# A hash-masked attention and gated MLP kernel: in 24 of 32 heads, VectorE instead of a DMA copies the rows of q and k that stay in their partitions

## The chip, the cores and the metric

The kernel runs on one core of a Trainium2 chip. The metric is device time in microseconds; before the change it is 724.53 us, the median of three runs (722.87, 724.53 and 728.32). The engines are called PE (TensorE), DVE (VectorE), ACT (ScalarE), POOL (GpSimd) and SP (SyncE, which here only issues DMAs).

## The reference

Four batches of eight heads, 768 positions, head dimension 64. A row of q may attend to those rows of k alone whose six-bit hash is the same; a row with no such partner attends to all of them alike. The attended heads of a batch go through a gated MLP with a spatial mixing matrix.

```python
q_bits = (np.einsum('bhsd,dk->bhsk', q, proj) > 0)          # 6 bits; k alike
mask = q_bucket[:, :, :, None] == k_bucket[:, :, None, :]
scores = np.where(mask, scale * (q @ k.T), -1e9)
attn = softmax(scores);  x = attn @ v                        # (B, S, H*D)
h = np.maximum(x @ w_in, 0);  u, v = h[..., :512], h[..., 512:]
v_n = (v - mean(v)) / sqrt(var(v) + 1e-6)
v_s = np.einsum('ts,bsd->btd', w_spatial, v_n) + b_spatial[None, :, None]
return (u * v_s) @ w_out
```

## The kernel before, in words

Every operand of a matmul that needs float32 accuracy is split into two float16 parts, high and low, and products of the parts are summed. Heads are numbered n = 0 to 31 and come in pairs p = n // 2, e = n % 2: one pair's q and k lie over each other in the 128 partitions, head e = 0 in partitions 0 to 63 and head e = 1 in 64 to 127.

For each pair, `load_qk` fetches k and q (768 KB), `hash_rows` makes the sign bits `sg` on PE and DVE, and `split_qk` writes the tile `hl`, four planes of 768 float16: q low, k high, q high, k low (L187 on ACT, L188 and L189 on DVE). There is one buffer for `hl`, so the split of the next pair waits until all that reads it is done.

For each head, `build` stacks these into one of four tiles `ab` of four planes: planes 0 and 1 hold q low over q high and k high over k low, so that one matmul over 128 partitions gives both cross products; planes 2 and 3 hold k high and q high in 64 partitions, and below them 12 rows of sign bits, with zeros (and in plane 2 a constant) under them. The rows of `ab` are brought by DMAs from SBUF to SBUF: one of 384 KB with the head's own 64 rows of four planes into partitions 0 to 63 (L210), one of 192 KB with two planes into partitions 64 to 127 (L211), and four small ones with the sign bits (L200), in the heads by queries from ACT's queue.

Heads 1 to 7 are done by keys (transposed scores, with a bound per row from `row_max` and its row 127 of `ab`); heads 0 and 8 to 31 by queries. A head by queries takes six steps of 128 queries. In a step, PE makes the scores (L291, L292), DVE takes the minimum of the negated scores into `nb` (L293), ACT the exponential (L294) and its float16 part (L297), DVE or POOL the rest (L298), SP issues a DMA transpose of the 384 KB `pp` into `pt` (L300), and PE multiplies by v (L313 to L315), at most five steps behind the scores. `normalize` and `transpose_x` end a head and a pair, and the MLP of a batch follows in 28 units that are spread over the 48 steps of the next batch; the last batch's MLP runs after the last step.

The order on each engine is set by a planner, which places instructions by the priority that `at(g, k)` gives and by its own timeline. In step g = 6n + i, `scores(n, i)` comes first; at i = 0, `build(n + 2)` is traced with priority 300 behind it, and what it puts on SP's queue is placed behind the last transpose (`tc.issue_after(st["tr"])`). `split_qk` of the pair after that comes at i = 3 of the odd head. SP's queue works in order: transposes, builds, loads, weights and outputs all pass through it.

Of the kernel before, what the change touches and what calls it, by code (L numbers as in the profile page):

```python
# [19 lines left out]
P = 128  # L20
D = 64
NB = 6
# [14 lines left out]
def lsh_attention_spatial_gating(  # L37
# [11 lines left out]
    nc = tc.nc  # L49
    B, NPAIR, _, _, S = kq.shape  # L50
    NH = 2 * NPAIR
    NT = S // P
    HS = S // 2
# [25 lines left out]


    NAB = 4
    NR = D + 2 * NB
    ab = [const.tile([P, 4, S], F16, name=f"ab{i}") for i in range(NAB)]
    for i, t in enumerate(ab):
        eng = nc.vector if i % 2 else nc.gpsimd
# [106 lines left out]
    def build(n):  # L192
        p, e = divmod(n, 2)
        hl, sg, t = st["hl", p], st["sg", p], ab[n % NAB]
        r = slice(D * e, D * e + D)
        q_s, q_h = (BQ_S[n >= NH], BQ_H[n >= NH])
        if n < 1:
            nc.sync.dma_start(out=t[0:D, 2:4], in_=hl[r, 1:3])
        for j in range(4):
            q_s.dma_start(  # L200
                out=t[D:NR, 3 - j // 2, (j % 2) * HS:(j % 2 + 1) * HS],
                in_=sg[32 * j + 16 * e:32 * j + 16 * e + 2 * NB, :])
        if n < 1:
            q_h.dma_start(out=t[0:D, 0:2], in_=hl[r, 0:2])
        else:

            top = hl[r, 0:2]
            (ps, pn), (ss, sn), (es, en) = top.ap
            src = replace(top, ap=[(ps, pn), (ss, 2), (ss, 2), (es, en)])
            q_h.dma_start(out=t[0:D].rearrange("p (a b) s -> p a b s", b=2), in_=src)  # L210
        q_h.dma_start(out=t[D:P, 0:2], in_=hl[r, 2:4])  # L211

    def split_v(p):
        if not has_queries(p):
# [40 lines left out]
    def scores_k(n, i):  # L255
        t = ab[n % NAB]
        ps = ps_sc.tile([P, 2, 512], F32, tag="sc", name=f"sp{n}_{i}")[:, :, :HS]
        ks = slice(i * P, (i + 1) * P)
        for c in range(2):
            cs = slice(c * HS, (c + 1) * HS)  # L260
            nc.tensor.matmul(ps[:, c], lhsT=t[:, 1, ks], rhs=t[:, 0, cs], start=True, stop=False)
            nc.tensor.matmul(ps[:, c], lhsT=t[:, 2, ks], rhs=t[:, 3, cs], start=False, stop=True)
        ex = wk.tile([P, S], F32, tag="pt", bufs=PTB, name=f"ex{n}_{i}")
        st["ex", n, i] = nc.scalar.activation(ex.rearrange("p (c q) -> p c q", c=2), ps, AF.Exp, scale=ISQ).ins
        st["pt", n, i] = ex
# [11 lines left out]
    def scores(n, i):  # L277
        if n in KEYS:
            scores_k(n, i)
            return  # L280
        t = ab[n % NAB]
        if i == 0:
            st["nb", n] = wk.tile([P, NT], F32, tag="nb", bufs=3, name=f"nb{n}")
        nb = st["nb", n][:, i:i + 1]
        ex = wk.tile([P, 2, HS], F32, tag="ex", bufs=EB, name=f"ex{n}_{i}")
        jk = ex.rearrange("p c k -> p (c k)").bitcast(BF16)[:, 0:S].rearrange("p (c k) -> p c k", c=2)
        qs = slice(i * P, (i + 1) * P)
        ps = ps_sc.tile([P, 2, 512], F32, tag="sc", name=f"sp{n}_{i}")[:, :, :HS]
        for c in range(2):
            cs = slice(c * HS, (c + 1) * HS)  # L290
            nc.tensor.matmul(ps[:, c], lhsT=t[:, 0, qs], rhs=t[:, 1, cs], start=True, stop=False)  # L291
            nc.tensor.matmul(ps[:, c], lhsT=t[0:P - 1, 3, qs], rhs=t[0:P - 1, 2, cs], start=False, stop=True)  # L292
        nc.vector.tensor_scalar(jk, ps, -ISQ, None, op0=ALU.mult, op1=ALU.min, accum_out=nb)  # L293
        st["ex", n, i] = nc.scalar.activation(ex, ps, AF.Exp, bias=nb, scale=ISQ).ins  # L294
        at(NT * n + i + G_H, 50)
        pp = wk.tile([P, 2, 2, HS], F16, tag="pp", bufs=PB, name=f"pp{n}_{i}")
        nc.scalar.copy(pp[:, 0], ex)  # L297
        (nc.gpsimd if i in (PL_POOL if n >= 2 * NH else PL_POOL1) else nc.vector).tensor_tensor(out=pp[:, 1], in0=ex, in1=pp[:, 0], op=ALU.subtract)  # L298
        pt = st["pt", n, i] = wk.tile([P, 2 * NT, P], F16, tag="pt", bufs=PTB, name=f"pt{n}_{i}")
        st["tr"] = nc.sync.dma_start_transpose(out=pt, in_=pp.rearrange("p g c k -> p (g c k)")).ins  # L300
# [183 lines left out]
    def at(g, k):  # L484
        tc.cur_priority = int(1000 * (g + 40) + k)
# [4 lines left out]
    hash_rows(0)  # L490
    split_qk(0)
    build(0)
    load_qk(1)
    build(1)
    load_v(0)
    at(-1, 0)
# [6 lines left out]
    for g in range(N * NT + LAG):  # L503
        n, i = divmod(g, NT)
        if n < N:
            at(g + G_S, 0)
            scores(n, i)
            r = n // 2
            at(g + G_P, 300)
# [17 lines left out]
            if i == BI and n + 2 < N:  # L527
                build(n + 2)
# [18 lines left out]
        while wv < N * NT and wv + (LAGK if wv // NT in KEYS else LAG) <= g:  # L547
            m, j = divmod(wv, NT)
# [64 lines left out]
```

## Time and profile before

| | |
|---|---|
| median of three runs | 724.53 us |
| the profiled execution, device time | 729.71 us |
| its span, first to last instruction | 727.9 us |
| granted PE clock, mean | 0.957 |
| busy: PE, DVE, ACT, POOL | 622.9, 520.4, 434.2, 326.6 us |
| DMA, bytes moved | 120.96 MB |
| DMA transposes of `pp` | 150 |
| DMAs of 384 KB into `ab` | 31 |

The profile comes from one execution. "Busy" of PE is modelled, since matmuls overlap; the DMA share is the mean busy share of 16 engines and can pass 1 where packets overlap. A wait is put down to what ended it last. Heads by keys fill about 49 to 165 us of the span, heads 8 to 31 about 165 to 650 us, and the last MLP the rest.

### The profile page before, as it was taken

The page shows a single profiled execution, that of the slowest core. Times are in us where ns is not written, and L with a number is a line of the kernel's source. Part 1 is how long each engine was busy: PE and PEld are TensorE (multiplying, and loading weights), DVE is VectorE, ACT ScalarE, POOL GpSimd, SP SyncE. Part 2 cuts the span into 40 slices and gives each one's busy share as a digit, 9 for nine tenths or more (in the row PEclk, how much of TensorE's full clock was granted, in tenths as well). Part 3 has the DMA queues.
Part 4 walks back from the last instruction along what each step waited for, and adds up shares of the span by engine and source line. Part 5 has one row for each costly group of instructions (what it writes and reads, how often), then busy time and mean ns, then how long its engine had stood idle before and what let it go on. Part 6 is the DMA issues. An engine that isn't in the chain of part 4 may idle for free. (4 is left out here: it accounts for less than half of the span.)

```text
span 727.9 us, 14930 instructions
## 1 busy us (share of the span) xinstructions
PE 622.9 (86%) x5759; PEld 393.2 (54%) x5759; DVE 520.4 (71%) x945; ACT 434.2 (60%) x668; POOL 326.6 (45%) x324
## 2 busy tenths in 40 slices
PE   1569897997987876998898899898989888999997
PEld 0237676875554543555555555565555555654553
DVE  4677894537899999768689887778699685845100
ACT  1345674356888677656667666667677677634221
POOL 5122542134479755446316672446146462441603
PEclk9969997999999988999999999999999999999999
DMA  9674745315999999997999999999999899860011
GB/s 238 151 140 146 170 132 105 94 47 131 233 247 210 212 198 203 218 210 161 223 213 186 193 202 183 228 197 206 228 227 169 167 168 210 147 157 10 1 44 44
DMA packets 290013, 120.96 MB, mean 166 GB/s; under 512 B 270741, under 2 KB 273813, under 8 KB 289941
## 3 DMA queue, kind: packets, MB, share of 16 engines
q1 hardware_dynamic: 287636, 119.11, 77.9%
q10 hardware_dynamic: 2304, 0.89, 0.5%
q8 instruction: 45, 0.74, 0.4%
q14 instruction: 28, 0.22, 0.1%
HBM read 28.33 MB, written 6.29 MB: 48 GB/s over the span
## 5 line engine op out<-in xcount | busy, mean ns | idle before, releaser
L294 ACT ACTIVATE ex<-sp,nb 128x768 f32<-128x768 f32 x150 | 134.6, 900 | 95.3 <-DVE ex L293 91.2
L293 DVE TENSOR_SCALAR_CACHE_REDUCE ex<-sp 128x768 bf16<-128x768 f32 x150 | 141.8, 949 | 43.2 <-PE sp L292 42.4
L298 DVE TENSOR_TENSOR pp<-ex,pp 128x768 f16<-128x768 f32 x116 | 125.9, 1091 | 20.7 <-ACT pp L297 20.5
L313 PE MATMUL pv<-vp,pt 128*128 128x65 f16 x900 | 105.5, 196 | 34.0 <-DMA pt<-pp 33.5
L291 PE MATMUL sp<-ab 128*128 128x384 f16 x300 | 102.2, 341 | 32.8 <-ACT ex L294 22.0
L297 ACT CAST pp<-ex 128x768 f16<-128x768 f32 x150 | 123.8, 830 | 10.6 <-ACT ex L294 2.5
L313 PEld LDWEIGHTS <-pt 128*128 128x128 f16 x900 | 85.4, 100 | 59.3 <-DMA pt<-pp 48.6
L298 POOL TENSOR_TENSOR pp<-ex,pp 128x768 f16<-128x768 f32 x34 | 58.2, 1711 | 123.9 <-ACT pp L297 101.1
L416 PE MATMUL sps<-ws,vn 128*128 128x384 f16 x576 | 103.9, 333 | 3.0 <-DVE sg L179 2.2
L314 PE MATMUL pv<-vp,pt 128*128 128x64 f16 x900 | 105.6, 195 | 0.0
L315 PE MATMUL pv<-vp,pt 128*128 128x65 f16 x900 | 105.3, 197 | 0.0
L292 PE MATMUL sp<-ab 127*128 127x384 f16 x300 | 102.4, 341 | 0.0
L314 PEld LDWEIGHTS <-pt 128*128 128x128 f16 x900 | 85.8, 99 | 10.7 <-issue 2.0
L315 PEld LDWEIGHTS <-pt 128*128 128x128 f16 x900 | 85.7, 99 | 3.7 <-issue 0.6
L416 PEld LDWEIGHTS <-vn 128*128 128x128 f16 x576 | 56.0, 100 | 40.7 <-issue 7.5
L431 PE MATMUL ops<-wo,g 128*128 128x512 f16 x288 | 70.0, 387 | 2.9 <-POOL wo L144 1.0
L401 PE MATMUL ups<-xt,wi 128*128 128x384 f16 x384 | 68.8, 331 | 0.0
L360 PE MATMUL vps<-wi,xt 128*128 128x512 f16 x288 | 67.1, 379 | 1.3 <-DMA xt<-xs 1.3
L332 POOL TENSOR_TENSOR x<-x,xf 128x384 f32<-128x384 f32 x32 | 36.8, 1151 | 69.7 <-DVE x L331 62.8
L274 PEld LDWEIGHTS pv<-vf,ex 128*128 128x128 f32 x504 | 65.6, 200 | 3.9 <-issue 1.1
L274 PE MATMUL pv<-vf,ex 128*128 128x65 f32 x504 | 64.5, 279 | 0.0
L421 POOL TENSOR_TENSOR sy<-sy,u 128x384 f32<-128x384 f32 x32 | 37.9, 1183 | 40.3 <-DVE sy L420 36.8
(87 smaller groups left out, 1006.1 us busy)
## 6 DMA issues: line engine op xcount, KB each, us to landing
qk<-kq SPq DMA_DIRECT2D x16, 768.0 KB
ab<-hl SPq DMA_DIRECT2D x31, 384.0 KB
ab<-hl SPq DMA_DIRECT2D x34, 192.0 KB
out<-o SPq DMA_DIRECT2D x24, 256.0 KB
v<-v SPq DMA_DIRECT2D x13, 384.0 KB
raw<-w_in SPq DMA_DIRECT2D x16, 256.0 KB
pt<-pp SPq DMA_TRANSPOSE x150
raw<-w_sp SPq DMA_DIRECT2D x12, 192.0 KB
```

The lines of the kernel that those rows point to most:

```text
L274: nc.tensor.matmul(acc[:, qi, :], lhsT=ex[:, qi * P:(qi + 1) * P], rhs=vf[p % 2][:, 2 * i + e, :], start=(i == 0 and qi == 0), stop=(i == ...
L291: nc.tensor.matmul(ps[:, c], lhsT=t[:, 0, qs], rhs=t[:, 1, cs], start=True, stop=False)
L292: nc.tensor.matmul(ps[:, c], lhsT=t[0:P - 1, 3, qs], rhs=t[0:P - 1, 2, cs], start=False, stop=True)
L293: nc.vector.tensor_scalar(jk, ps, -ISQ, None, op0=ALU.mult, op1=ALU.min, accum_out=nb)
L294: st["ex", n, i] = nc.scalar.activation(ex, ps, AF.Exp, bias=nb, scale=ISQ).ins
L297: nc.scalar.copy(pp[:, 0], ex)
L298: (nc.gpsimd if i in (PL_POOL if n >= 2 * NH else PL_POOL1) else nc.vector).tensor_tensor(out=pp[:, 1], in0=ex, in1=pp[:, 0], op=ALU.subtract)
L313: nc.tensor.matmul(acc, lhsT=pt[:, c, :], rhs=vh, start=(i == 0 and c == 0), stop=False)
L314: nc.tensor.matmul(acc[:, 0:D], lhsT=pt[:, c, :], rhs=vl, start=False, stop=False)
L315: nc.tensor.matmul(acc, lhsT=pt[:, NT + c, :], rhs=vh, start=False, stop=(i == NT - 1 and c == NT - 1))
L416: nc.tensor.matmul(ps[:, :HS], lhsT=vn[gv][:, c, d * P:(d + 1) * P], rhs=ws[gw][:, c, hs], start=(k == 0), stop=(k == 3 * NT - 1))
L431: nc.tensor.matmul(ps, lhsT=gt[h][gg][:, c, j * P:(j + 1) * P], rhs=wo[gw][:, c, :], start=(k == 0), stop=(k == 3 * NF - 1))
```

## The change

In the heads by queries from head 8 on (`near`), the head's own 64 rows stay in the partitions in which `hl` has them. Two DVE copies of 64 partitions by 1536 float16 bring the four planes there (k high and q high into planes 2 and 3; q low and k high into planes 0 and 1), and the DMA of 384 KB is gone. The two planes for the other half of the partitions are still brought by a DMA of 192 KB, and the sign bits by four small ones; in odd heads these now go to the lower half, since the head's own rows are in the upper half. For that the lower half of planes 2 and 3 of the two tiles that odd heads use is set to zero once by POOL, at heads 9 and 11, and the matmul of planes 3 and 2 takes all 128 partitions in odd heads. Head 0 and the heads by keys are built as before, and the minima are taken as before.

```diff
-    NR = D + 2 * NB
...
         q_s, q_h = (BQ_S[n >= NH], BQ_H[n >= NH])
+        near = n >= NH
+        z = D - D * e if near else D
+        if near and e and n < NH + NAB:
+            nc.gpsimd.memset(t[0:D, 2:4, :], 0.0)
...
             q_s.dma_start(
-                out=t[D:NR, 3 - j // 2, (j % 2) * HS:(j % 2 + 1) * HS],
+                out=t[z:z + 2 * NB, 3 - j // 2, (j % 2) * HS:(j % 2 + 1) * HS],
                 in_=sg[32 * j + 16 * e:32 * j + 16 * e + 2 * NB, :])
...
+        elif near:
+            nc.vector.tensor_copy(t[r, 2:4], hl[r, 1:3])
+            nc.vector.tensor_copy(t[r, 0:2], hl[r, 0:2])
         else:
...
-        q_h.dma_start(out=t[D:P, 0:2], in_=hl[r, 2:4])
+        q_h.dma_start(out=t[z:z + D, 0:2], in_=hl[r, 2:4])
...
+        K = P if n % 2 and n >= NH else P - 1
...
-            nc.tensor.matmul(ps[:, c], lhsT=t[0:P - 1, 3, qs], rhs=t[0:P - 1, 2, cs], start=False, stop=True)
+            nc.tensor.matmul(ps[:, c], lhsT=t[0:K, 3, qs], rhs=t[0:K, 2, cs], start=False, stop=True)
```

## The prediction

> **What bounds the kernel now.** I read the busy shares and the DMA row of the page first, then the chain that ended last, then the stretches between 165 and 650 us, in which the heads by queries run, and last the waits there.
>
> ```profile
> span 727.9 us, 14930 instructions
> PE 622.9 (86%) x5759; PEld 393.2 (54%) x5759; DVE 520.4 (71%) x945; ACT 434.2 (60%) x668; POOL 326.6 (45%) x324
> DMA  9674745315999999997999999999999899860011
> PE 14%; DMA 5%; POOL 4%; DVE 4%; issue 3%; ACT 2%; SPq 0%; ACTq 0%; POOLq 0%; DVEq 0%
> ...
> 490.83 0.24 POOL fl L323
> ...
> 520.47 4.86 DMA ab<-hl
> 525.35 1.49 ACT hl L187
> ...
> 653.02 3.29 DMA xt<-xs
> ```
>
> No engine is full over the span, and the DMA engines are full in nearly every slice in which queries run. The chain is known from 490.83 us on. Behind 653 us + 3.29 it is PE alone, the last MLP, which the change doesn't touch. Between 490.8 and 653 us, 162 us long, it changes hands all the time; the 4% of DVE are 29 us, so DVE holds 18% of that part (29 / 162), and once it runs through a DMA into `ab` for which ACT waited.
>
> ```profile
> core 0: us, PE busy (x) PEld busy (x) DVE busy (x) ACT busy (x) POOL busy (x), PEclk, DMA share, GB/s
> 50.00:165.00 115.00, 103.02 (x781) 82.41 (x780) 75.83 (x160) 59.75 (x106) 36.48 (x53) 0.93 0.47 117
> 165.00:650.00 485.00, 424.51 (x4451) 262.38 (x4449) 399.14 (x710) 337.78 (x504) 250.24 (x222) 0.96 0.98 198
> 200.00:300.00 100.00, 77.05 (x821) 47.27 (x820) 97.43 (x163) 76.68 (x133) 69.18 (x59) 0.93 1.03 214
> 375.00:400.00 25.00, 22.00 (x256) 14.18 (x254) 24.76 (x49) 18.73 (x32) 12.96 (x12) 1.00 0.94 197
> ```
>
> From 165 to 650 us DVE is busy 399.14 of 485 us (82%), PE 424.51 (88%), the DMA engines 0.98. In two stretches of 125 us together, DVE is busy 122.2: there each microsecond put on DVE lengthens the program. In the other 360 us DVE has 83 us of idle time.
>
> ```profile
> ACT ex L294 <- DVE ex L293: 77.2, 62, 3.6
> PEld L313 <- DMA pt<-pp: 40.8, 39, 3.8
> DVE ex L293 <- PE sp L292: 39.6, 29, 3.6
> PE sp L291 <- ACT ex L294: 22.0, 16, 2.6
> ...
> SPq L300 <- DVE pp L298: 71.9, 50, 6.2
> ...
> ACT hl L187 <- DMA ab<-hl: 8.7, 6, 2.2
> ```
>
> These are the waits between 165 and 650 us. PE waits for transposed `pt` 40.8 us in 39 of 144 steps: the largest wait of the engine that ends the program. SP waited for DVE's `pp` before 50 of the 144 transposes; the other 94 had their data ready (65%) and came when SP's queue let them. So the path through SP and the DMA engines, which the change relieves, and DVE, which it loads, are both near the limit.
>
> **The change, part by part.** *The DMA of 384 KB goes, in 24 heads.*
>
> ```profile
> L210 SPq DMA_DIRECT2D ab<-hl x22: 602/632/1488, 175.0 to 597.3; - x22
> ...
> L210 SPq DMA_DIRECT2D ab<-hl x2: 631/820/1010, 125.4 to 139.8; - x2
> ...
> ab<-hl SPq DMA_DIRECT2D x31, 384.0 KB
> ab<-hl SPq DMA_DIRECT2D x34, 192.0 KB
> ...
> 447.06 1.45 SPq L300 DMA_TRANSPOSE pt<-pp  x1
> ...
> 481.03 0.60 SPq L211 DMA_DIRECT2D ab<-hl  x1
> 481.80 2.79 SPq L300 DMA_TRANSPOSE pt<-pp  x1
> ...
> 500.69 0.60 SPq L211 DMA_DIRECT2D ab<-hl  x1
> 501.46 3.27 SPq L300 DMA_TRANSPOSE pt<-pp  x1
> ```
>
> Its issue takes SP 0.63 us (median). Further, a transpose that SP issues just behind a build takes 2.79 and 3.27 us to issue, against 1.45 us without one: 1.34 and 1.82, mean 1.58 us, in which the queue is still emptying. Of the 576 KB of a build 384 go, so I take two thirds, 1.05 us. SP's queue gains 0.63 + 1.05 = 1.68 us a head, 37 us over the 22 builds between 165 and 650 us (the two builds of such heads before, at 125 and 140 us, count nothing). As a cross-check, the DMA engines moved 117 GB/s at a share of 0.47 in the first stretch, 249 GB/s when full, which makes 1.58 us of 384 KB.
>
> How much of this reaches PE? I looked at the steps behind three builds.
>
> ```profile
>   PEld L313: 2.0, 1
> ...
>   PEld L313: 1.0, 1
> ```
>
> These are the waits on transposes issued at 464 to 471 us and at 501 to 505 us, both just behind a build; the one issued at 481.80 had no wait for it. With at most 1.68 us to be had at each, that is 1.68, 1.0 and 0: mean 0.89 us, times 22 heads 20 us, half of the 40.8 us. Its bounds are 0, if `pp` comes late instead, and 37 us. ACT's waits for these DMAs at L187 (8.7 us) shrink by two thirds, 5.8 us; ACT is busy 337.78 of 485 us and takes most of that up, so I count 2 us. Together **-22 us**.
>
> *Two DVE copies come, in 24 heads, 48 in all.* The trace has no such copy. The nearest row is L181, a DVE operation from float16 in SBUF to float16 in SBUF; L331 and L298 give the price of an operation that goes element by element.
>
> ```profile
> L181 DVE TENSOR_SCALAR sg<-sg,hc 128x384 f16<-128x384 f16 x16 | 8.9, 558 | 0.2
> L181 DVE TENSOR_SCALAR sg<-sg,hc x16: 302/320/1093, 11.2 to 560.0; 128x384 f16<-128x384 f16 x16
> L331 DVE TENSOR_TENSOR x<-pv,rv 128x384 f32<-128x384 f32 x32 | 17.7, 552 | 0.6
> L298 DVE TENSOR_TENSOR pp<-ex,pp x116: 921/954/1933, 34.2 to 643.9; 128x768 f16<-128x768 f32 x116
> L298 POOL TENSOR_TENSOR pp<-ex,pp x34: 1632/1646/2356, 26.3 to 632.9; 128x768 f16<-128x768 f32 x34
> ```
>
> 384 more elements cost 954 - 552 = 402 ns, 1.05 ns each, with 150 ns fixed. L181 takes 320 ns, 170 above the fixed part; four times as many elements make 680 + 150 = 0.83 us. At 1.05 ns an element the copy would take 1.76 us, the upper end; as the lower end I take 0.55 us, the 552 ns of L331, which has a quarter of the elements. L181's mean lies 0.24 us over its median, and its longest is 1.09 us: something holds it up at times. Operations of POOL last up to 1.65 us, and POOL is busy 250 of the 485 us. I take 0.83 + 0.24 = 1.07 us a copy, by the row most alike: 2.14 us a head, 47 us over 22 heads.
>
> The Trainium skill, VectorE: DVE Perf Modes, section "The perf-mode tier table", has 693 ns for a 16-bit copy of 2048 elements in SBUF; with its four elements a cycle that makes some 0.56 us here, an estimate from that page, and the sum below would be 5 us lower. Its page SBUF — State Buffer, section "Who interferes with whom", speaks against the change: such a copy needs a port pair that it shares with GpSimd, the one that comes second waits for the whole of the other's instruction. By that rule L181's longest time is a wait for POOL, which the trace allows, and POOL would wait for the copies too; the 0.24 us hold DVE's side of it.
>
> What does it cost? Five of the builds lie in the two stretches in which DVE is full (four from 200 to 300 us, one from 375 to 400):
>
> ```profile
> L210 SPq DMA_DIRECT2D ab<-hl x4: 627/632/802, 212.1 to 280.7; - x4
> ...
> L210 SPq DMA_DIRECT2D ab<-hl x1: 637/637/637, 380.5 to 380.5; - x1
> ```
>
> There 5 x 2.14 = 10.7 us count in full. Of the other 17 x 2.14 = 36.4 us I count DVE's share of the chain, 18%: 6.5 us. Together **+17 us**. If DVE's idle time is no cover at all, it is 47 us.
>
> *Behind the copies* stand DVE's minimum and difference of the next steps, which ACT, POOL and SP wait for (77.2 us of ACT's waits are for L293 already). They land on the steps whose transposes wait for SP now, so part of their delay is spent where the data lay ready anyway; that is why I don't charge them in full. The copies themselves wait for nothing: `hl` was split some three steps before, and the tile was last read by the head two before. L187 of the next split now waits for the odd head's copies as well, three steps later, which is covered.
>
> *Small parts.* Two fills by POOL, of heads 9 and 11:
>
> ```profile
> L86 POOL MEMSET ab<- 64x1536 f16 x2 | 2.7, 1374 | 0.1
> L291 PE MATMUL sp<-ab 128*128 128x384 f16 x300 | 102.2, 341 | 32.8 <-ACT ex L294 22.0 <-DMA ab<-hl 9.5 <-DVE mx L242 1.2
> L292 PE MATMUL sp<-ab 127*128 127x384 f16 x300 | 102.4, 341 | 0.0
> ```
>
> Each is the shape of L86, 1.37 us. The odd head's sign DMAs wait for it on ACT's queue, and ACT's exponentials stand behind them, for these two heads alone; POOL's queue may hold another 1.65 us. I count 0, with 3 us at most. The matmul over 128 rows costs what that over 127 does (341 ns each). The sign DMAs are as many and as large as before.
>
> The sum is -22 + 17 = **-5 us**: 724.7 us for the profiled execution, whose time was 729.7 (the span and 1.8 us around it). That execution was 5.2 us above the median of the runs, so for the median it makes 719.5 us, which I round to 720.
>
> **The rivals.** *The queue is the limit* (faster). What speaks for it: 65% of the transposes found their data ready, and the DMA share is 0.98. Then 65% of the 37 us of queue time reach PE, 24 us, and 2 us of ACT's; and with so much slack behind DVE its 47 us cost only the 18%, 8 us: -18 us, 706. Against it: DVE's full stretches, in which a shorter queue brings nothing.
>
> *DVE becomes the bound* (slower). From 165 to 650 us DVE is busy 399.1 us and waits 39.6 us for scores, which leaves 46.3 us; over the 44 copies, that is 1.05 us each. From there on, each further microsecond of a copy lengthens the stretch. At 1.5 us, between L181's price and the upper end, it is 66 - 46.3 = +20 us, 744; at 1.2 us, +6.5 us, 731. For it: my own price stands at this point. Against it: the 39.6 us of waits for scores shrink where PE waits less for `pt`.
>
> *An even exchange* (no change). The delay moves from SP's queue to DVE, in the same steps, and PE waits as long as before: 0 us, 724.5. For it speaks that a transpose starts at the later of SP and `pp`, and that 50 of 144 wait for `pp` already. My forecast lies near it. That the change does nothing at all is excluded by the DMA rows, since 24 transfers go.
>
> **The numbers.** A difference under 1%, 7.2 us, is about what a measurement of this kernel can't tell from none. Forecast and even exchange, both within 1%: 0.39 together (0.22 and 0.17). The queue as the limit, and what of the forecast's spread passes -7 us: 0.37. DVE as the bound, and an order of the planner that puts the copies ahead of urgent minima: 0.24. The range is 703 to 738: below, the first rival less the 3 us by which runs scatter; above, DVE as the bound at about 1.35 us a copy (59 - 46 = +13). Both signs hold much of the chance; the forecast alone spans 714 to 727.
>
> **What the profile after would show.** 7 DMAs of 384 KB into `ab` instead of 31; transposes behind a build issued in about 2 us instead of 2.8 to 3.3; PE's waits for `pt` near 20 us instead of 40.8; 48 copies of 0.55 to 1.2 us; DVE over 90% busy from 165 to 650 us. The forecast is wrong if the copies take over 1.2 us, if SP's waits for `pp` grow as much as its issues shrink, or if PE's waits for `pt` nearly vanish.

## The result, and the profile after

The changed kernel takes 730.4 us (median of 20 runs), the kernel before 727.47 us in 20 runs beside them. The ratio is 1.0066, with a 95% interval of 1.0038 to 1.0095: slower by 0.66%, some 5 us, where I had forecast 0.6% faster. Ratios, here and below, are taken over the fast runs alone, so this one is a little larger than the 2.9 us between the two medians would make it. The interval does not contain "no change", though the size is within the 1% I had called hard to tell. The profiled execution after took 730.83 us.

From the page of the kernel after: its span, the busy times, the DMA share in 40 slices, the chain that ended last, and the two kinds of DMA into `ab`.

```profile
span 729.0 us, 14947 instructions
PE 627.9 (86%) x5759; PEld 395.7 (54%) x5759; DVE 554.2 (76%) x993; ACT 434.2 (60%) x668; POOL 329.4 (45%) x326
DMA  9674644115969688694998978997987688860011
PE 16%; POOL 3%; DMA 3%; issue 2%; DVE 2%; ACT 1%; SPq 0%; POOLq 0%
...
ab<-hl SPq DMA_DIRECT2D x34, 192.0 KB
ab<-hl SPq DMA_DIRECT2D x7, 384.0 KB
```

The 24 transfers are gone and the DMA engines are no longer full. PE issues the same 5759 matmuls and is busy 5 us longer; DVE 33.8 us longer. The stretch of the heads by queries, and the two parts of it in which DVE was full (window, then busy us of PE, its weight loads, DVE, ACT and POOL, the granted clock, the DMA share and GB/s):

```profile
165.00:650.00 485.00, 427.81 (x4441) 263.42 (x4440) 429.89 (x751) 337.39 (x503) 251.06 (x223) 0.95 0.85 180
200.00:300.00 100.00, 74.94 (x735) 44.31 (x734) 97.79 (x163) 69.87 (x121) 66.83 (x58) 0.85 0.79 176
375.00:400.00 25.00, 20.75 (x213) 11.70 (x206) 23.73 (x49) 17.05 (x25) 7.15 (x7) 0.94 0.93 175
```

Between 200 and 300 us PE finished 735 matmuls instead of 821, its clock granted 0.85 instead of 0.93. The waits from 165 to 650 us (us, times, longest):

```profile
ACT ex L301 <- DVE ex L300: 84.8, 60, 4.7
...
PEld L320 <- DMA pt<-pp: 36.1, 38, 4.1
...
DVE ex L300 <- PE sp L299: 20.6, 21, 4.4
PE sp L298 <- ACT ex L301: 20.1, 18, 2.8
...
SPq L307 <- DVE pp L305: 119.6, 64, 7.4
```

PE's waits for `pt`, of which I expected half to go, fell by 4.7 us only. SP's waits for DVE's `pp` rose from 71.9 to 119.6 us, ACT's for DVE's minimum from 77.2 to 84.8. SP's queue itself did become free. Behind two builds of the kernel after (start, us to issue):

```profile
484.99 0.58 SPq L217 DMA_DIRECT2D ab<-hl  x1
485.73 1.44 SPq L307 DMA_TRANSPOSE pt<-pp  x1
...
504.83 0.59 SPq L217 DMA_DIRECT2D ab<-hl  x1
505.63 1.85 SPq L307 DMA_TRANSPOSE pt<-pp  x1
```

The 18 transposes that come next behind a build in SP's queue, from 165 to 650 us, took 2.94 us to issue in the median before and 1.57 after. The copies were cheaper than I had priced them (busy us, mean ns of one, idle time before them):

```profile
L209 DVE COPY ab<-hl 64x1536 f16<-64x1536 f16 x24 | 19.3, 803 | 0.2
L210 DVE COPY ab<-hl 64x1536 f16<-64x1536 f16 x24 | 18.2, 758 | 1.9 <-PE sp L267 1.7
```

A copy took 0.55 us in the mean where no operation of POOL ran at the same time (27 of the 48), and 1.08 us where one did (21).

So the relief is there and the price is lower than forecast, yet the sum has the other sign. DVE's own order of time (start, us) shows where the copies went:

```profile
198.17 0.94 DVE L187 SCALAR_TENSOR_TENSOR hl<-qk,hl 128x768 f16<-128x768 f32 x1
199.03 1.76 DVE L188 SCALAR_TENSOR_TENSOR hl<-qk,hl 128x768 f16<-128x768 f32 x1
200.71 1.18 DVE L209 COPY ab<-hl 64x1536 f16<-64x1536 f16 x1
201.82 0.17 DVE L376 BATCH_NORM_AGGREGATE mv<-bs 128x2 f32<-128x6 f32 x1
202.01 1.07 DVE L209 COPY ab<-hl 64x1536 f16<-64x1536 f16 x1
203.12 1.56 DVE L305 TENSOR_TENSOR pp<-ex,pp 128x768 f16<-128x768 f32 x1
204.60 1.84 DVE L210 COPY ab<-hl 64x1536 f16<-64x1536 f16 x2
206.47 0.96 DVE L300 TENSOR_SCALAR_CACHE_REDUCE ex<-sp 128x768 bf16<-128x768 f32 x1
```

The planner doesn't place two copies at each head's `build`. In eleven of the twelve pairs all four come close behind the split of that pair, about steps 3 to 5 of an odd head: they are done 3 to 9 us after its last operation starts, with two minima or `pp` between them at most. From 198.17 to 206.44 us, over 8 us, DVE makes one `pp` and no minimum. What PE does meanwhile (columns as above):

```profile
202.60:206.00 3.40, 3.40 (x47) 1.95 (x42) 3.35 (x4) 1.04 (x2) 2.85 (x3) 1.00 0.01 3
206.00:209.40 3.40, 1.59 (x24) 1.01 (x23) 3.34 (x7) 1.33 (x4) 0.00 (x0) 1.00 0.51 116
209.40:219.70 10.30, 6.54 (x40) 3.28 (x37) 10.13 (x24) 8.36 (x14) 6.63 (x5) 0.50 0.95 217
219.70:230.00 10.30, 9.21 (x115) 6.28 (x114) 9.45 (x15) 9.65 (x19) 9.71 (x10) 1.00 0.97 206
```

PE still has work until 206 us; the DMA engines, with no `pp` to transpose, are empty (0.01). Then PE works 1.59 of 3.40 us, and its clock is granted at 0.50 for the next 10.3 us: 40 matmuls, where the same time behind it holds 115. The stop that the burst brings is followed by a longer stretch at half clock.

### The profile page after: what moved, and what is told of

Its sections match the earlier page's. It is cut to its first block, busy times and chain, and to the rows that moved or that the text cites. A ratio compares the mean times of both kernels' runs of the same rounds, so it can differ in the third digit from the quotient of the medians.

```text
span 729.0 us, 14947 instructions
## 1 busy us (share of the span) xinstructions
PE 627.9 (86%) x5759; PEld 395.7 (54%) x5759; DVE 554.2 (76%) x993; ACT 434.2 (60%) x668; POOL 329.4 (45%) x326
## 5 line engine op out<-in xcount | busy, mean ns | idle before, releaser
L305 DVE TENSOR_TENSOR pp<-ex,pp 128x768 f16<-128x768 f32 x116 | 127.4, 1102 | 18.8 <-ACT pp L304 18.3
L320 PE MATMUL pv<-vp,pt 128*128 128x65 f16 x900 | 106.8, 197 | 28.6 <-DMA pt<-pp 28.1
L298 PE MATMUL sp<-ab 128*128 128x384 f16 x300 | 104.2, 347 | 30.9 <-ACT ex L301 20.1
L322 PE MATMUL pv<-vp,pt 128*128 128x65 f16 x900 | 106.7, 198 | 0.0
L423 PE MATMUL sps<-ws,vn 128*128 128x384 f16 x576 | 102.3, 331 | 4.6 <-DVE sy L427 4.6
L299 PE MATMUL sp<-ab 127*128 127x384 f16 (+1 forms) x300 | 104.6, 349 | 0.0
```

What stands on the lines that cost most here:

```text
L299: nc.tensor.matmul(ps[:, c], lhsT=t[0:K, 3, qs], rhs=t[0:K, 2, cs], start=False, stop=True)
L320: nc.tensor.matmul(acc, lhsT=pt[:, c, :], rhs=vh, start=(i == 0 and c == 0), stop=False)
L322: nc.tensor.matmul(acc, lhsT=pt[:, NT + c, :], rhs=vh, start=False, stop=(i == NT - 1 and c == NT - 1))
L423: nc.tensor.matmul(ps[:, :HS], lhsT=vn[gv][:, c, d * P:(d + 1) * P], rhs=ws[gw][:, c, hs], start=(k == 0), stop=(k == 3 * NT - 1))
```

## The experiments

My theory after the result: the relief is as large as forecast; the copies cost what they do because four of them close together (the "burst" below) hold back the minima and differences on which ACT, SP and so PE depend, where I had thought them covered. The rivals: it is only DVE's total load, wherever the copies stand; the copies block GpSimd at a port they share; or the planner's new order of everything else costs the time. Ratios are to the kernel before, with 95% intervals; 1% is 7.27 us, and differences in us are worked out from the ratios. Where two kernels are compared, the ± joins their intervals.

**Without the copies.**

```diff
         elif near:
-            nc.vector.tensor_copy(t[r, 2:4], hl[r, 1:3])
-            nc.vector.tensor_copy(t[r, 0:2], hl[r, 0:2])
+            pass
```

> The changed kernel without its 48 VectorE copies: the own rows of the heads by queries from head 8 on are not brought at all (they keep what lay there), so that neither the 384 KB DMA nor the copies run; all else is the same. It shows what the DMA was worth by itself, and, against the changed kernel, what the copies cost. Theory A (VectorE's load: the relief is real and the copies eat it): ratio to the kernel before 0.970 to 0.980, 15 to 22 us faster. Theory B (the four copies of a pair stand in one burst behind its split; their place costs more than their load): also 0.970 to 0.980. Theory C (the DMA was hidden and PE's waits for pt come from elsewhere): 0.995 to 1.005, and the copies then cost some 5 us.

Measured: 708.77 us, ratio 0.9762 [0.9707, 0.9816], that is -17.3 us. The relief, then, is real and near my 22 us, and the copies take 22 us (3.04% ± 0.6) for the 37.5 us that they last. Without them, ACT's waits for DVE are down by 29 us from the kernel after:

```profile
ACT ex L300 <- DVE ex L299: 55.5, 52, 2.7
PEld L319 <- DMA pt<-pp: 32.1, 28, 4.9
```

**Each copy twice.**

```diff
             nc.vector.tensor_copy(t[r, 2:4], hl[r, 1:3])
             nc.vector.tensor_copy(t[r, 0:2], hl[r, 0:2])
+            nc.vector.tensor_copy(t[r, 2:4], hl[r, 1:3])
+            nc.vector.tensor_copy(t[r, 0:2], hl[r, 0:2])
```

> The changed kernel with each copy made twice, so that 37 us more of VectorE time stand in the same places. Theory A: each further microsecond of VectorE costs about as much as the first ones, so 15 to 25 us over the changed kernel, ratio to the kernel before 1.027 to 1.04. Theory B: a burst of eight costs more than twice a burst of four: over 1.04. Theory C: 3 to 8 us over the changed kernel, ratio 1.01 to 1.018.

Measured: 753.58 us, 1.037 [1.0322, 1.0418]. The second set costs 22 us again (3.04% ± 0.6). There was no cover for the first set that the second has used up: as far as two points can tell, the cost runs straight from the first copy on. The copying lasts 65.1 us in all, 27.7 more (0.68 us a copy in the mean), so a microsecond of the second set costs more, not less.

**The copies spread.** One behind the minimum of step 1, one behind that of step 2, of the head two before.

```diff
+    def own_rows(n, d, s):
+        p, e = divmod(n, 2)
+        r = slice(D * e, D * e + D)
+        nc.vector.tensor_copy(ab[n % NAB][r, d:d + 2], st["hl", p][r, s:s + 2])
...
+            if i in (1, 2) and NH <= n + 2 < N:
+                with (tc.issue_after(st["mn", n, i]) if n not in KEYS else ExitStack()):
+                    own_rows(n + 2, *((2, 1) if i == 1 else (0, 0)))
```

> The changed kernel with its copies spread: one copy behind the minimum of step 1 and one behind that of step 2 of the head two before, so that no two copies stand next to each other and none stands behind the split. Theory A: the load is the same, so the time is that of the changed kernel, ratio 1.003 to 1.010. Theory B: PE's waits at the steps 0, 4 and 5 fall back to what they were before the change, and the relief of SP's queue stays: ratio 0.980 to 0.993. Theory C: 0.998 to 1.006.

Measured: 723.62 us, 0.9953 [0.9922, 0.9984]. This lies between the ranges of the theories. The copies are as many and as large, and the kernel takes 8 us less (1.13% ± 0.4). But they also last less, 31.7 us in all instead of 37.5 (0.78 us in the mean beside an operation of POOL, not 1.08); at 22 us for 37.5 that makes 3.4 of the 8 us. The rest points at the place, and the kernels in the old order, below, show it. PE's waits for `pt` end below those of the kernels so far (before 40.8, after 36.1, without copies 32.1). That wait, and the group of the copies:

```profile
PEld L324 <- DMA pt<-pp: 28.7, 27, 2.9
...
L221 DVE COPY ab<-hl 64x1536 f16<-64x1536 f16 x48 | 31.5, 660 | 2.4 <-PE sp L271 1.7
```

**The copies on ScalarE, and on GpSimd.** The second kernel has `nc.gpsimd.tensor_copy` at the same place.

```diff
-            nc.vector.tensor_copy(t[r, 2:4], hl[r, 1:3])
-            nc.vector.tensor_copy(t[r, 0:2], hl[r, 0:2])
+            nc.scalar.copy(t[r, 2:4], hl[r, 1:3])
+            nc.scalar.copy(t[r, 0:2], hl[r, 0:2])
```

> The changed kernel with the 48 copies on ScalarE, whose copy of as many elements takes about 1.5 us (its cast of 1536 float32 does): some 70 us more on an engine that was busy 70% of the time from 165 to 650 us, and nothing more on VectorE. Theory A: VectorE is relieved, ScalarE has the room: 0.980 to 0.995. Theory B: the burst stands on ScalarE instead and holds up the exponentials by 6 us each pair: 1.000 to 1.015. Theory C: 0.995 to 1.005.

> The changed kernel with the 48 copies on GpSimd, where a fill of as many elements took 1.37 us: 65 to 80 us more on an engine that was busy 52% of the time from 165 to 650 us. Theory A: VectorE loses the load, GpSimd has the room: 0.980 to 0.995. Rival (GpSimd's operations hold VectorE's two-input operations up, and its own differences and sums of x come late): 1.000 to 1.020.

Measured: 757.02 us, 1.0429 [1.0372, 1.0486], and 792.24 us, 1.0867 [1.082, 1.0914]. Both are slower than any theory had it. One copy lasts 1467 ns on ScalarE and about 1850 on GpSimd. The rows of the kernel with ScalarE, groups first, then waits:

```profile
L210 ACT COPY ab<-hl 64x1536 f16<-64x1536 f16 x24 | 35.2, 1467 | 0.0
```

```profile
PEld L320 <- DMA pt<-pp: 62.0, 40, 3.8
```

ScalarE is less busy than DVE (337 against 430 of 485 us in the kernel after), and yet its 70 us of copies cost 48 us over the kernel without copies. And this is no burst of four: by its trace, the planner put them on ScalarE two by two, some 20 us apart. An engine's spare time over the stretch doesn't say what more work on it costs.

**Fills instead of copies.** As in the kernel without copies, but DVE makes a fill that reads nothing for each, behind the split, as long as a copy with nobody in its way.

```diff
-            nc.vector.tensor_copy(t[r, 2:4], hl[r, 1:3])
-            nc.vector.tensor_copy(t[r, 0:2], hl[r, 0:2])
+            with tc.issue_after(st["s2", p]):
+                nc.vector.memset(spare[r], 0.5)
+                nc.vector.memset(spare[r], 0.5)
```

> The kernel without copies and without the 384 KB DMA, with a fill of 64x560 float16 by VectorE in a spare tile in place of each copy, placed behind the split as the copies are. A fill of 768 elements took 698 ns in the profile, so each should take about 0.55 us, the copy's shortest time, and reads nothing. It leaves out the own rows of the heads from 8 on. Theory A1 (what counts is VectorE's time alone): 26 us at 0.6, 16 us over the kernel without copies (0.976): 0.992 to 1.002. Theory A2 (what counts is the copy's way through a port shared with GpSimd: its waits, 0.23 us each of 0.78, and GpSimd's): under 0.987.

Measured: 745.36 us, 1.0238 [1.0195, 1.0281], 35 us above the kernel without copies and outside both ranges. The fills last less than the copies, and read nothing:

```profile
L211 DVE MEMSET spare<- 64x560 f16 x24 | 12.6, 525 | 2.8 <-issue 1.9 <-DVE spare L211 0.2
```

They cost more than the copies, so what a copy reads isn't the cause. But planned anew the fills may stand elsewhere, and this needed the four kernels that follow.

**The order of before, held.** In all kernels so far the planner had also reordered everything else: going by tile and shape, 3833 of PE's 5759 matmuls stand in the same place of its order after the change. In the next four, every engine is tied to its order in the kernel before; the copies go in behind the split of their pair (or spread as above), the 24 DMAs are gone. The order of the matmuls in all four traces is that of the kernel before, 5759 of 5759. In 6 of the 12 pairs the four copies behind a split stand in a row; in the others a minimum comes between the even head's two and the odd head's two, in some with more beside it. With relief alone and with fills, the own rows are left out.

```diff
+        info = mybir.DependencyInfo(mybir.DependencyClass.NoSync, mybir.DependencyReason.DATA)
+        for a, b in zip(order, order[1:]):
+            tc.add_manual_dep(b, a.name, info, reason="order")
...
+            if WORK in ("copies", "spread"):
+                i = nc.vector.tensor_copy(t[r, d:d + 2], hl[r, s:s + 2])
+            elif WORK == "fills":
+                i = nc.vector.memset(spare[r], 0.5)
```

> The instructions of every engine held in the order that the planner gave the kernel before; the 24 DMAs of 384 KB are gone and nothing brings the own rows of the heads from 8 on (they are left out). It is the relief of SP's queue by itself, without a new plan. Theory A (relief and load are both real, the plan matters little): as in the freshly planned kernel without copies, 0.971 to 0.982. Theory P (a good part of what was seen is the planner's new order): 0.985 to 1.000.

> The whole change in the order of the kernel before: the four copies of a pair stand behind its split on VectorE (those of the odd head not before the last minimum of the head that used the tile), everything else in the old order. Theory A: the same as the changed kernel, 1.000 to 1.012, that is some 20 us over the kernel with the relief alone. Theory P (the new order is what cost the gain): 0.983 to 0.995.

> As f2_copies_old_order, with a fill of 64x560 float16 of 0.53 us in a spare tile in place of each copy, in the same places (the own rows from head 8 on are left out). Theory A1 (VectorE's time is what costs): 25 us of fills and some 6 us of gaps at 0.6: 18 us over f1_relief_old_order, nearly as slow as f2_copies_old_order. Theory A2 (the port that the copies share with GpSimd is what costs): under 8 us over f1_relief_old_order. Theory P: the earlier run with fills, 35 us over the kernel without copies, owed its time to its plan, so in the old order it is within 10 us of f1_relief_old_order.

> As f2_copies_old_order, with the copies spread: one behind the minimum of step 1, one behind that of step 2 of the head two before. Theory A: the same as f2_copies_old_order, within 0.4%. Theory B (bursts): 5 to 10 us faster than f2_copies_old_order, 0.99 to 1.00 of the kernel before, or less.

| in the old order | us | ratio | against relief alone |
|---|---|---|---|
| relief alone, no copies | 705.99 | 0.9714 [0.9668, 0.9759] | |
| copies behind the split | 732.8 | 1.0103 [1.0047, 1.0159] | +28.3 us (± 5) |
| fills behind the split | 740.57 | 1.0176 [1.0131, 1.022] | +33.6 us (± 5) |
| copies spread | 721.16 | 0.9924 [0.9893, 0.9955] | +15.3 us (± 4) |

Waits from 165 to 650 us, of relief alone, of copies behind the split and of copies spread, in this order. (The profiled execution of the second took 740.86 us, the longest of its six, so its rows overstate the mean.)

```profile
ACT ex L355 <- DVE ex L354: 67.8, 55, 3.6
...
PE sp L352 <- ACT ex L355: 20.7, 14, 2.9
...
PEld L374 <- DMA pt<-pp: 19.6, 24, 2.4
...
SPq L361 <- DVE pp L359: 79.7, 48, 7.0
```

```profile
ACT ex L355 <- DVE ex L354: 88.9, 58, 5.0
...
PE sp L352 <- ACT ex L355: 33.9, 22, 5.4
...
PEld L374 <- DMA pt<-pp: 22.3, 22, 2.4
...
SPq L361 <- DVE pp L359: 105.5, 60, 8.4
```

```profile
ACT ex L355 <- DVE ex L354: 72.8, 65, 3.6
...
PE sp L352 <- ACT ex L355: 25.7, 17, 3.0
PEld L374 <- DMA pt<-pp: 26.3, 30, 3.1
...
SPq L361 <- DVE pp L359: 102.7, 57, 7.4
```

Three things follow. First, the relief alone is 20.8 us, and PE's waits for `pt` fall to 19.6 us, as the prediction said. Copies make SP wait longer for `pp` (26 us more in a burst, 23 spread), but the burst brings back hardly any of PE's waits for `pt` (22.3). What grows on PE's side is another wait: ACT waits 21 us more for the minimum, and PE 13 us more for ACT to have read the scores, so that their PSUM buffer is free. Spread, both grow by 5 us only.

Second, the place counts: the same copies, 33.7 us in all behind the split and 32.4 us spread, differ by 13 us (± 5) in price, which is almost half of what the burst costs. Spread, they still cost 15.3 us, so the load by itself costs as well. Spreading changes two things at once, how many stand together and behind which instruction; no run takes these apart.

Third, the new order isn't to blame: in the old one the burst comes out at 1.0103, after the change with the new one at 1.0066.

The fills bear on the port. They last 25.2 us, with 6.9 us of gaps in between, and each takes 525 ns, whether an operation of POOL runs beside it (25 of them) or not (23), where the copies beside one are held up (in this order to 0.89 us, from 0.55):

```profile
L268 DVE MEMSET spare<- 64x560 f16 x48 | 25.2, 525 | 6.9 <-DVE spare L268 3.9 <-issue 2.0 <-PE pv L376 0.2
```

These 32 us of DVE's time cost 33.6, more than any theory had; the copies in the same places, 33.7 us in all, cost 28.3. Waits of copies and POOL for each other lengthen the copies, then, but they aren't needed to explain the cost; being on DVE at that place is enough.

**DVE relieved elsewhere.** On top of the spread copies (planned anew), the subtraction that makes the low part of x, or the difference `pp` of step 5, goes to GpSimd: one line of the diff in each kernel.

```diff
-    XL_ENG = nc.vector
+    XL_ENG = nc.gpsimd
...
-    PL_POOL = (2,)
+    PL_POOL = (2, 5)
```

> The kernel with the spread copies, and the low part of x (a VectorE operation of 0.64 us mean, once a head) on GpSimd. Theory A (each microsecond of VectorE counts about 0.6 of itself, as the copies and their doubling showed: 22 us for 37 us): 32 operations, 20 us less on VectorE, 12 us less: ratio to the kernel before 0.975 to 0.985. Rival (GpSimd, with 52% busy and the last in the chain of x, becomes late): 0.995 to 1.010.

> The kernel with the spread copies, and in the heads from 16 on a second of the six differences of p (step 5) on GpSimd instead of VectorE: 16 operations of 0.95 us or more go from VectorE, 16 of 1.7 us come to GpSimd. Theory A: 15 to 17 us less on VectorE, some 9 us less: 0.980 to 0.990. Rival (the longer operation delays pp, and GpSimd's operations hold up VectorE's copies): 0.995 to 1.010.

Measured: 0.9972 [0.9937, 1.0006] and 0.998 [0.9956, 1.0004], against 0.9953 for the spread alone. Taking load off DVE brought nothing, as the rivals had it. With the copies out of the way of the minima, DVE's load is not what the next microsecond depends on, or GpSimd gives back what DVE gains; these two runs don't tell which.

## Why the prediction was wrong, point by point

*The relief, 22 us: right.* Held to the old order it is 20.8 us, planned anew 17.3. The working had a somewhat low queue term (a transpose behind a build gained 1.37 us in the median, where I took 1.05) and a share reaching PE that was about right.

*The price of a copy, 1.07 us: too high by over a third.* It measured 0.80 and 0.76 us. Of its two parts, the 0.24 us for being held up was right: the mean of 0.78 lies 0.23 above the 0.55 us of a copy with no operation of POOL beside it. The 0.83 us was wrong: the row nearest in kind, L181, gave too much when scaled by elements. The Trainium skill, VectorE: DVE Perf Modes, section "The perf-mode tier table", from which I had worked out 0.56 us, fits the copies that nothing holds up; the mean lies 0.2 us above it. (With 0.56 us the sum would have been 8 us lower, or 4 us with the 0.24 us on top, not 5.) This error alone would have made the forecast too slow.

*"Of the other 17 x 2.14 = 36.4 us I count DVE's share of the chain, 18%": this step failed.* With the measured price the same working gives 5 x 1.56 + 18% of 17 x 1.56 = 12.6 us; the copies cost 22 us as planned, 28.3 in the old order. That is 59% and 84% of their own duration, not 37%. Shown is that the place is a good part of it: the step took one copy to be like another, while the planner made bursts, and in the old order the burst costs 13 us more than the same copies spread. Spread, at 15.3 us (13.9 planned anew), they cost near the 12.6; whether the 18% is right there or fits by luck, no run says. The rest is argued: the share of the chain is what DVE holds on average, and an instruction pushed ahead of DVE's urgent work isn't in the average place; and the share counts the direct delay, not what PE loses when it stops (below).

*"They land on the steps whose transposes wait for SP now": wrong.* They land behind the split, about steps 3 to 5 of the odd head. I had read that `build` is traced at step 0, and took its place in the program for its place in time; but the copies wait for little but the split (the odd head's also for the last scores from their tile), and the planner took them about as soon as they could run. By my own count over the trace, PE's waits for `pt` did fall where the transposes had waited, in steps 1 to 3, from 33.3 to 12.4 us; in step 0 they rose from 4.0 to 14.9 and in steps 4 and 5 from 3.6 to 8.7. The gain was had and given back at other steps.

*Which waits would show it.* I had argued with DVE's delay of `pp`, SP and `pt`. The old order's rows show the other way round, minimum, exponential, PSUM buffer, scores, of which I had quoted the first wait (77.2 us) without charging it. One sign that I had named for a wrong forecast did come: SP's waits for `pp` grew by 47.7 us, more than the 37 us that its queue was to gain. Another that I had expected did not: DVE is busy 429.89 of 485 us, 89%, and not over 90%.

*The rivals.* "DVE becomes the bound" had the right side and, at 1.2 us a copy, the right time (731), but not the mechanism: it needed copies over 1.05 us, and at 0.78 us DVE still waits 20.6 us for scores. Cost began with the first copy and not at a threshold, as the doubled copies show. "An even exchange" comes nearest in kind: the delay did move from SP's queue to DVE, only not in the same steps and not for nothing. In "the queue is the limit", the relief of 26 us was some 5 us too high, and the price for the copies 14 us or more too low. It also rested on a misreading: that the 94 transposes for which SP didn't wait for DVE's `pp` "had their data ready" and came when the queue let them. Further rows of the same view of the kernel before have SP waiting for PE, 64 times, so not all of the 94 were held by the queue:

```profile
SPq L300 <- PE pv L315: 48.4, 40, 3.7
SPq L300 <- PE sp L292: 31.6, 24, 2.6
```

*The small parts.* The two fills by POOL, the sign DMAs and the matmul over 128 rows are all within relief alone. Its -20.8 us is near the -22 without any cost of them; no run prices them by themselves.

What would have been a gain is the spread: 721.16 us, 0.9924 [0.9893, 0.9955], in the old order, the best of the kernels here that do the whole work.

## What to carry to other kernels

When work moves from a queue to an engine, price it where it will stand in that engine's order, and look at what is queued behind it; the engine's idle share over a stretch is no cover for a burst. A planner may place ready work with no deadline about as early as it can run, as it did here on DVE, so tie it behind the urgent instruction of a step, one piece at a time. Two runs, one with the removed part alone and one with the added part doubled, give both terms of the sum at once.

## What the runs showed of the hardware

PE's clock turns a short stop into a longer one. In the trace it is granted at 1.00 or 0.50 in stretches of 3.41 us. I counted, over all fourteen profiles between 165 and 650 us, how the clock of a stretch follows from PE's idle time in the one before: under 0.5 us idle, half clock in none of 1378; 0.5 to 1 us, in 14 of 229; 1 to 1.5 us, in 18 of 138; 1.5 to 2 us, in 50 of 107; 2 us and more, in 108 of 109. The burst at 206 us, above, is one such case: 1.81 us idle (1.73 of it in one gap), then three stretches at half clock. The Trainium skill, TensorE: Matmul & The Clock Gate, section "HAM oscillation — how this bites in real kernels", says to leave no idle gap over about 3.4 us; here gaps of half that, inside one stretch, were enough.

In the old order, the time at half clock between 165 and 700 us is 27.3 us with relief alone, 54.6 with the burst and 34.1 with the copies spread. PE's busy time on the pages of these three moves alike, for the same 5759 matmuls (relief, burst, spread):

```profile
PE 616.2 (88%) x5759; PEld 393.2 (56%) x5759; DVE 524.4 (75%) x945; ACT 433.4 (62%) x668; POOL 332.6 (47%) x326
```

```profile
PE 634.4 (86%) x5759; PEld 402.4 (54%) x5759; DVE 547.9 (74%) x993; ACT 433.8 (59%) x668; POOL 331.9 (45%) x326
```

```profile
PE 621.0 (86%) x5759; PEld 394.9 (55%) x5759; DVE 549.4 (76%) x993; ACT 434.5 (60%) x668; POOL 340.3 (47%) x326
```

At half clock, score matmuls of 128x384 that follow each other start 320 ns apart instead of 162. So the 27 us more would cost PE up to 13.7 us, of the 28.3 that the burst costs. These are single executions. By the granted clock that every run lists, the mean time at half clock over the whole execution is 54 us with relief alone, 82 with the burst and 70 with the copies spread (68 in the kernel before, 74 after the change): the spread kernel's profile shows less of it than its runs do.

That the stop comes first and the half clock after is seen in the order of the stretches. The clock isn't all of the cost: the kernel after the change and the one with its copies spread spend the same time at half clock (51.2 us in both profiles from 165 to 700 us, 74 us in the mean of the runs of both), and are 8 us apart. How the rest of the cost divides between DVE's delay and the clock stays open, as does why the fills cost 5 us (± 5) more than the copies.
